# Gated mix on one core: halves of the tokens' tiles joined, spill, zero stores and weight loads moved

## The chip, the core and the metric

The kernel runs on one core of a Trainium2 chip. The metric is device time in microseconds. The kernel before took 444.37 us (median of 3 runs, 443.2 to 444.62).

Engines are named as in the profile: PE is the matmul engine (PEld its weight loads), DVE the vector engine, ACT the scalar engine, POOL the GpSimd engine, SP the engine that here issues every DMA. Each takes its instructions in order; a "q" behind the name (SPq, DVEq) is its queue.

## The reference

For 2048 tokens x of width 448, a gate mixes a sliding, dilated attention with a squared-ReLU MLP:

```python
g = sigmoid((x * gate_w).sum(-1, keepdims=True))
# attention: 16 heads of 28; query s sees keys s, s-2, ..., s-14
q, k, v = split(x @ wqkv)
a = (softmax(mask(q . k[s - 2*w]) * 28**-0.5) @ v) @ wo
# MLP, hidden width 1792
b = relu(x @ w1 + b1)**2 @ w2 + b2
out = g * a + (1 - g) * b
```

## The kernel before

**High and low parts.** PE multiplies in fp32r. To keep accuracy each operand is split in two: ACT rounds it to a high part (L101), DVE subtracts that from the original for the low part (L102), and a product takes three matmuls (high x high, high x low, low x high). The 448 rows of a contraction are three tiles of 128 and one of 64; the last 64 rows are stored twice, so that their parts share a tile. A chunk of 512 tokens therefore has eight tiles of x, `x0` to `x7`, each 128 x 512: high and low of three row tiles, and `x7`, `x8` for the rest (`X`, L113).

**Stage A, q, k, v.** Four chunks. The first (`qkv_first`, L235) runs while its weights still arrive, behind warm-up matmuls on a tile of zeros (L482). The others go through `qkv_two` (L262) twice each. Two products of 64 rows run side by side in the halves of PE; when an accumulator changes halves, a `turn` (L177) writes one element of its PSUM tile, by ACT (L182) or DVE (L184), which orders the two halves' matmuls. A finished accumulator is evacuated by ACT into a stage tile (L193, ring of `ST_BUFS = 3`); when two token tiles are in it, SP stores it to DRAM (`q_d`, `k_d`, `v_d`, L199).

**Spill.** The x tiles of chunks 0, 1 and 2 are stored to `x_d` (`x_spill`, L127) and loaded again in stage B (`x_reload`, L604) into a ring of `RING` buffers, of which `RING - 8` are loaded ahead of a chunk's end and the rest as its last matmuls free them.

**Attention** runs beside PE's work: POOL multiplies (L306 for q with k, L313 for weights with v), DVE reduces (L307, L319), ACT takes the exponential. Its q, k and v come from DRAM, shifted by the halo; rows before the first token are zeros, stored by `halos` (L540) from a tile `halo0`. Products go through a ring of `PP_BUFS = 4` tiles.

**Stage B, the MLP.** Chunks in the order 3, 0, 1, 2. For each of 14 hidden tiles f: eleven matmuls (`mlp_h`, L620), ACT's ReLU and squares (L626 to L628), DVE's low part hl (L629), and, two f later, twelve matmuls with w2 (`mlp_o`, L684). From the third chunk on, the attention output is transposed (L702, L703), split, and multiplied by wo (`wo_tr`, `wo_mm`, L725), one token tile per f as long as there are any; the last eight come in the tail.

**Order of work.** One Python program emits all engines' instructions, so what it emits first stands first in each engine's queue. A planner's clock counts PE's matmuls (`advance`, L431); `when(t, ...)` and `at(dt, ...)` put a load or a split at a time of this clock, in nanoseconds. `SPLIT_AT` sets the splits of the x chunks, `ATT_DELAY` when attention's first step is emitted after its loads. w1 arrives in four pieces (`w1_piece`, L454), w2's first seven rows in two (`w2_piece`), the other seven and wo row by row in stage B (`w2_row`, `wo_row`). The raw pieces of stage A share two buffers (`raw_tile`).

## Time and profile before

| | us |
|---|---|
| runs (3): lowest, median, highest | 443.2, 444.37, 444.62 |
| the profiled execution | 443.05 |
| its span | 441.3 |
| PE idle before an instruction, in the middle of the span | 3.6, 0.5 and 0.4 |

The page gives busy times per engine and the span in 40 slices of 11 us, of which these rows show the course:

```profile
PE   8969999999999999999999999999999999999996
DVE  4412312297899997776655677652857766663453
POOL 1000000784999899999898897843699998692000
PEclk9998999999999999999999999999999999999999
DMA  6899499979481304723203472210353600400013
```

A digit is the busy share in tenths. PE is busy nearly throughout, with a dip in the third slice; PEclk, the clock that PE was granted, dips in the fourth. DMA is busy above all in the first eleven slices, stage A. POOL begins with attention in the eighth and is done five slices before the end.

The DMAs that the change touches (out<-in, queue, count, KB each, median us from issue to landing):

```profile
x_d<-x SPq DMA_DIRECT2D x24, 256.0 KB, 7.3
q_d<-st SPq DMA_DIRECT2D x8, 448.0 KB, 6.0
w1raw<-w SPq DMA_DIRECT2D x4, 896.0 KB, 8.4
k_d<-st SPq DMA_DIRECT2D x8, 448.0 KB, 3.6
```

### The profile page before, as it was taken

What the parts mean: (1) busy time and instruction counts of PE and PEld (TensorE: products, weight loads), DVE (VectorE), ACT (ScalarE), POOL (GpSimd) and SP (SyncE); (2) the same over time, 40 slices, a digit from 0 to 9 for tenths busy, and PEclk for the clock granted to TensorE, in tenths of its full rate; (3) what the DMA queues carried; (4) which work ended last, traced back from release to release, by engine and by line L of the source; (5) the groups of instructions that cost most, each with busy time, mean ns of one, the idle gap of its engine ahead of it and who ended that gap; (6) DMA issues with size and microseconds to landing.
All of it is one profiled execution on the core that took longest, in us unless ns stands there. A gap on an engine that the chain in (4) does not pass through costs nothing.

```text
span 441.3 us, 6590 instructions
## 1 busy us (share of the span) xinstructions
PE 431.4 (98%) x2516; PEld 386.1 (87%) x2516; DVE 268.0 (61%) x384; ACT 178.6 (40%) x372; POOL 276.3 (63%) x167
## 2 busy tenths in 40 slices
PE   8969999999999999999999999999999999999996
PEld 7859999999888888888888888988888888888995
DVE  4412312297899997776655677652857766663453
ACT  4533453334475453344333552425333334333630
POOL 1000000784999899999898897843699998692000
PEclk9998999999999999999999999999999999999999
DMA  6899499979481304723203472210353600400013
GB/s 179 274 366 338 138 367 311 345 262 304 148 285 54 120 1 121 272 80 120 78 1 120 144 273 88 95 42 22 127 196 102 224 1 0 142 0 0 2 62 126
DMA packets 36623, 65.44 MB, mean 148 GB/s; under 512 B 3056, under 2 KB 26608, under 8 KB 36208
## 3 DMA queue, kind: packets, MB, share of 16 engines
q1 hardware_dynamic: 36592, 65.02, 43.2%
q8 instruction: 20, 0.33, 0.3%
q14 instruction: 11, 0.09, 0.1%
HBM read 41.23 MB, written 23.77 MB: 147 GB/s over the span
## 4 chain that ended last, share of the span: by engine, by line
PE 86%; DMA 5%; POOL 4%; DVE 2%; issue 1%; SPq 1%; ACT 1%; DVEq 0%; POOLq 0%; ACTq 0%
PE b L684 31%; PE h L620 30%; PE qkv L174 13%; PE a L725 8%; POOL qk L306 4%; DMA x_d<-x 2%; PE qkv L242 2%; DMA k<-k_d 1%; DMA q_d<-st 1%; PE oT L702 1%; PE warm L485 1%; DVE w2al L102 1%; SPq L502 1%; DVE lg L307 0%; ACT st L193 0%
## 5 line engine op out<-in xcount | busy, mean ns | idle before, releaser
L306 POOL TENSOR_TENSOR qk<-q,k 128x896 f32<-128x896 f32 x64 | 140.5, 2230 | 102.3 <-DMA k<-k_d 84.2
L313 POOL TENSOR_TENSOR av<-lg,v 128x896 f32<-128x896 f32 x64 | 122.6, 2018 | 13.3 <-DVE o L319 6.6
L626 ACT ACTIVATE h<-h,b1t 128x512 f32<-128x512 f32 x56 | 37.0, 661 | 164.9 <-PE h L620 164.9
L174 PE MATMUL qkv<-wqh,x 64*128 64x448 f32 (+1 forms) x528 | 88.3, 369 | 4.1 <-DVE qkv L184 3.6
L629 DVE TENSOR_TENSOR hl<-h,hh 128x512 fp32r<-128x512 f32 x56 | 38.5, 688 | 59.0 <-ACT h L628 58.9
L307 DVE TENSOR_REDUCE lg<-qk 128x32 f32<-128x896 f32 x64 | 67.1, 1076 | 0.5 <-POOL qk L306 0.5
L174 PEld LDWEIGHTS qkv<-wqh,x 64*128 64x128 f32 x528 | 60.7, 188 | 6.7 <-DVE qkv L184 4.3
L319 DVE TENSOR_REDUCE o<-av 128x112 f32<-128x896 f32 x64 | 66.4, 1073 | 0.1
L174 PE MATMUL qkv<-wql,x 64*128 64x448 f32 (+1 forms) x264 | 57.6, 368 | 0.0
L193 ACT ACTIVATE st<-qkv 128x448 f32<-128x448 f32 x48 | 24.7, 546 | 44.3 <-PE qkv L174 34.6
L684 PE MATMUL b<-w2ah,hl 128*128 128x448 f32 x112 | 40.7, 363 | 0.4 <-DVE hl L629 0.4
L684 PE MATMUL b<-w2bh,hh 128*128 128x448 f32 x112 | 41.0, 366 | 0.0
L684 PE MATMUL b<-w2bl,hh 128*128 128x448 f32 x112 | 40.9, 365 | 0.0
L684 PE MATMUL b<-w2bh,hl 128*128 128x448 f32 x112 | 40.9, 365 | 0.0
L684 PE MATMUL b<-w2ah,hh 128*128 128x448 f32 x112 | 40.7, 364 | 0.0
L684 PE MATMUL b<-w2al,hh 128*128 128x448 f32 x112 | 40.5, 362 | 0.0
L627 ACT ACTIVATE hh<-h 128x512 fp32r<-128x512 f32 x56 | 33.5, 599 | 3.6 <-DMA v_d<-st 1.8
L628 ACT ACTIVATE h<-h 128x512 f32<-128x512 f32 x56 | 33.2, 593 | 0.0
L174 PEld LDWEIGHTS qkv<-wql,x 64*128 64x128 f32 x264 | 31.8, 188 | 0.7
L620 PE MATMUL h<-x1b,w1h 128*128 128x512 f32 x84 | 28.6, 394 | 0.0
L620 PE MATMUL h<-x2b,w1h 128*128 128x512 f32 x84 | 28.5, 393 | 0.0
L620 PE MATMUL h<-x0b,w1h 128*128 128x512 f32 x84 | 28.4, 391 | 0.0
(108 smaller groups left out, 771.9 us busy)
## 6 DMA issues: line engine op xcount, KB each, us to landing
k<-k_d SPq DMA_DIRECT2D x8, 840.0 KB, 5.6
v<-v_d SPq DMA_DIRECT2D x8, 840.0 KB, 4.5
x_d<-x SPq DMA_DIRECT2D x24, 256.0 KB, 7.3
q_d<-st SPq DMA_DIRECT2D x8, 448.0 KB, 6.0
w1raw<-w SPq DMA_DIRECT2D x4, 896.0 KB, 8.4
k_d<-st SPq DMA_DIRECT2D x8, 448.0 KB, 3.6
v_d<-st SPq DMA_DIRECT2D x8, 448.0 KB, 6.9
q<-q_d SPq DMA_DIRECT2D x8, 448.0 KB, 3.4
```

The source lines that it names most:

```text
L174: nc.tensor.matmul(acc.pt[:, :acc.n], a[rows], w[rows], start=acc.todo == 21, stop=acc.todo == 1)
L306: nc.gpsimd.tensor_mul(pr, q[:, s:s + 1].to_broadcast([P, W, C]), k[:, s:s + W])
L307: pending.append(lambda: nc.vector.tensor_reduce(lg[:, s], pr.rearrange("p w (h d) -> p w h d", h=HG), axis=AX.X, op=ALU.add))
L313: nc.gpsimd.tensor_mul(pr.rearrange("p (h d) w -> p w h d", h=HG), lg[:, s][:, :, :, None].to_broadcast([P, W, HG, DH]), v[:, s:s + W].rea ...
L319: pending.append(lambda: nc.vector.tensor_reduce(o[:, g * C:(g + 1) * C], pr, axis=AX.X, op=ALU.add))
L620: nc.tensor.matmul(pt, w, a, start=i == 0, stop=i == len(pr) - 1)
L626: nc.scalar.activation(pt, pt, AF.Relu, bias=b1t[:, f:f + 1])
L627: nc.scalar.activation(hh, pt, AF.Square)
L628: nc.scalar.activation(pt, pt, AF.Square)
L629: at(HL_DELAY, lambda: nc.vector.tensor_sub(hl, pt, f32(hh)))
L684: nc.tensor.matmul(bps[tl][:, :D], a[:, sl], w, start=f == 0 and i == 0, stop=f == NF - 1 and i == 2)
L725: nc.tensor.matmul(pa[:, :D], a, w, start=i == 0, stop=i == len(pr) - 1)
```

## The change

- The high and the low part of a row tile of x lie in one tile, 128 x 2 x 512. A chunk has four tiles instead of eight, a spill four stores of 512 KB instead of eight of 256 KB, a reload four loads. `RING` is 5 of the new tiles instead of 10 of the old.
- Chunk 0's spill is emitted at 10.5 us of the planner's clock instead of 9, behind q's two stores on SP.
- The warm-up's `zero` lies in the ring of attention's products instead of in the buffer of k, to which k's weights are loaded.
- The zeros of the halo are stored by two DMAs instead of four, at 44.5 us instead of 16.
- w1's pieces, the biases and w2 come at other times; only four of w2's rows come in stage A, ten in stage B, one every 4.5 us instead of 3.2, and wo from 50 us into stage B instead of 26.
- `ATT_DELAY` is 20 us instead of 15.

```diff
-ATT_DELAY = 15000.0
+ATT_DELAY = 20000.0
-RING = 10
+RING = 5
-    x_d = tc.dram_tile([3, 8, P, CH], F32, name="x_d")
+    x_d = tc.dram_tile([3, 4, P, 2, CH], F32, name="x_d")
...
-            self.h, self.l = tiles[0:6:2], tiles[1:6:2]
-            self.x7, self.x8 = tiles[6:8]
+            self.h, self.l = [t[:, 0] for t in tiles[:3]], [t[:, 1] for t in tiles[:3]]
+            self.x7, self.x8 = tiles[3][:, 0], tiles[3][:, 1]
-        return X([pool.tile([P, CH], F32R, tag=f"x{j}", name=f"x{c}_{j}") for j in range(8)])
+        return X([pool.tile([P, 2, CH], F32R, tag=f"x{j}", name=f"x{c}_{j}") for j in range(4)])
...
-        split_full(raw[:, k], *(x.t[2 * k:2 * k + 2]))
+        split_full(raw[:, k], x.t[k][:, 0], x.t[k][:, 1])
     def x_spill(c, x):
-        for j in range(8):
+        for j in range(4):
             nc.sync.dma_start(x_d[c, j], f32(x.t[j]))
...
-    halo0 = smp.tile([G * HALO, C], F32, tag="lg", name="halo0")
+    halo0 = smp.tile([2 * G * HALO, C], F32, tag="lg", name="halo0")
...
-    zero = attp.tile([P, 2 * P], F32R, tag="k", name="zero")
+    zero = prodp.tile([P, 2 * P], F32R, tag="pp", name="zero", bufs=PP_BUFS)
...
-        for par in range(2):
-            for d in (k_d, v_d):
-                nc.sync.dma_start(d[par, :, 0:HALO], halo0)
+        for d in (k_d, v_d):
+            nc.sync.dma_start(d.rearrange("a g r c -> (a g) r c")[:, 0:HALO], halo0)
...
-    when(9000.0, x_spill, 0, x)
-    when(15000.0, w1_piece, 0, 13000.0)
-    when(16000.0, halos)
-    when(36500.0, w1_piece, 1, 10000.0)
-    when(48000.0, biases)
-    when(57500.0, w1_piece, 2, 11000.0)
-    when(67500.0, w1_piece, 3, 12000.0)
-    when(77500.0, w2_piece, 0, 4, w2ah, w2al, 0, 10000.0)
-    when(89000.0, w2_piece, 4, 3, w2ah, w2al, 0, 11000.0)
+    when(10500.0, x_spill, 0, x)
+    when(25000.0, w1_piece, 0, 13000.0)
+    when(44500.0, halos)
+    when(46500.0, w1_piece, 1, 12500.0)
+    when(67000.0, w1_piece, 2, 10500.0)
+    when(68000.0, w1_piece, 3, 17000.0)
+    when(70000.0, biases)
+    when(86000.0, w2_piece, 0, 4, w2ah, w2al, 0, 6500.0)
...
-        r = (8 * i + j) % RING
-        xt = (xpool if r < 8 else bp).tile([P, CH], F32R, tag=f"x{r}", name=f"x{c}b_{j}")
+        r = (4 * i + j) % RING
+        xt = (xpool if r < 4 else bp).tile([P, 2, CH], F32R, tag=f"x{r}", name=f"x{c}b_{j}")
...
-        at(5000.0, lambda: split_full(raw, w2bh[:, f - NFA], w2bl[:, f - NFA], soon))
+        at(5000.0, lambda: split_full(raw, *w2hl(f), soon))
...
-    for i in range(7):
-        at(i * 3200.0, lambda i=i: w2_row(NFA + i))
+    for i in range(4, NF):
+        at((i - 4) * 4500.0, lambda i=i: w2_row(i))
     for k in range(4):
-        at(26000.0 + k * 3200.0, lambda k=k: wo_row(k))
+        at(50000.0 + k * 4500.0, lambda k=k: wo_row(k))
...
-    early = RING - 8
+    early = RING - 4
...
-                nxt += [x_reload(i + 1, j) for j in range(early, 8)]
+                nxt += [x_reload(i + 1, j) for j in range(early, 4)]
```

## The prediction

> **What bounds the kernel now.** I read the page's busy times first, then PE's waits, then the chain of waits in order of time, and then the stretches around each wait.

> ```profile
> PE 431.4 (98%) x2516; PEld 386.1 (87%) x2516; DVE 268.0 (61%) x384; ACT 178.6 (40%) x372; POOL 276.3 (63%) x167
> ```

> PE is busy 431.4 of 441.3 us, and the change leaves its useful matmuls as they are. Only the 9.9 us in which PE is idle, and time in which it runs slowly, can be won. PE's waits:

> ```profile
> PE qkv L174 <- DVE qkv L184: 3.6, 1, 3.6
> PE warm L485 <- DVE zero L483: 1.2, 1, 1.2
> PE qkv L174 <- ACT qkv L182: 0.5, 1, 0.5
> PE b L684 <- DVE hl L629: 0.4, 1, 0.4
> ```

> The 3.6 us wait stands at 29.48 to 33.04. The chain says what it is made of (start, us, what):

> ```profile
> 15.08 8.74 DMA x_d<-x
> 23.88 5.67 DMA q_d<-st
> 30.09 0.97 ACT st L193 x2
> 31.07 0.53 ACT x L101
> 31.62 1.35 DVE x L102 x3
> 33.04 57.13 PE qkv L174 x536
> ...
> 121.44 2.55 DVE w2al L102
> 123.99 0.61 DVE hl L629
> ```

> Eight spill stores of chunk 0 hold the queue to 23.9, so q's first store is issued only then and lands at 29.6. ACT cannot evacuate k before that, for the stage ring has three buffers; behind that evacuation on ACT stand chunk 1's splits, behind those on DVE the memset of a turn, and PE waits for the memset. After the wait PE runs slowly for a while (columns: stretch, then busy time of PE, PEld, DVE, ACT, POOL, then the granted clock, DMA share, GB/s):

> ```profile
> 34.00:38.00 4.00, 4.00 (x28) 3.60 (x26) 0.22 (x3) 0.98 (x2) 0.00 (x0) 0.57 0.88 265
> ```

> At a clock of 0.57 over 4 us, 0.43 x 4 = 1.7 us of matmul time are lost. The half-microsecond wait belongs to another queue:

> ```profile
> SPq L502 <- PE warm L245: 5.4, 1, 5.4
> ```

> ```profile
> 16.31 0.58 ACT L101 ACTIVATE wqh<-wqraw 128x448 fp32r<-128x448 f32 x1 [1.15 <-DMA wqraw<-wqkv]
> ```

> SP waits 5.4 us to load k's weights, because the warm-up's `zero` lies in the buffer that they go to. They reach ACT late, and ACT's turn (L182), queued behind their split, is late for PE.

> **The change, part by part.** Times are sums against the profiled execution: 443.05 us, of which 441.3 are the span. That is 1.3 below the median of 444.37 shown; the forecast is moved by that difference at the end.

> *q's stores ahead of the spill.* q's two stores are then issued when ACT has evacuated them, at 17.5 to 18.9, not at 23.9. With the landing time of before, 5.67 us, the first lands near 23.2. From that landing to PE's restart the chain takes 33.04 - 29.57 = 3.5 us, so PE could go on at 26.7; it arrives at the turn at 29.5. The wait goes whole, with some 2.3 us to spare after the next item: 3.56 us, and with the idleness the slow stretch, 1.7 us. [...]

> What is late next is the spill itself: four stores of 512 KB, issued after q, with k's stores behind them on SP. The third stage buffer comes free for the last v tiles when k's first store has landed: issued near 25, landing after 4.4 us (median around there) to 8.7 us (the spills' median): 29 to 34. PE needs those PSUM tiles freed only 21 matmul pairs into chunk 1, at 32.5 + 21 x 0.205 = 36.8. Nothing is paid.

> *`zero` in another pool.* Eight loads are issued up to 5.4 us earlier (six of k's and v's weights, their last rows, then chunk 1's x). ACT's waits of 2.83 and 1.15 us for them end and PE's 0.53 us goes. They enter the queue behind the loads that PE needs first, and the one queue's packets start in order of issue in the trace, so those are not delayed: 0, bound +0.3 (PE's weight loads wait 0.3 us there now).

> *Pairs in one tile.* Spills and reloads become 12 issues each of 512 KB instead of 24 of 256 KB; the bytes stay. A reload of 256 KB lands in 3.3 to 5.0 us (medians), a 1 MB load in 8.0; 512 KB lies between, and I take 5. A slot comes free with the third matmul of a chunk's last h group and is needed at the fourth of the next: 8 x 0.227 + 36 x 0.2025 + 3 x 0.227 = 9.8 us. That hides it up to 9.8; without that cover each of three boundaries would pay the 5 us. The reloads stand on SP behind a q and a k load that wait for POOL; those go out some 10 us before them now (166.5 against 176.6).

> *Halos and biases.* Four zero stores become two and move behind chunk 2's spill; they must land before attention's first k load, at 72 now. Biases go 22 us later, still 35 us ahead of the first use at 118. Both cost nothing while the SP queue runs ahead as it does; SP's stores behind them wait for PE anyway.

> *Weights spread out.* w1's four pieces load 10, 10, 9.5 and 0.5 us later by the planner's clock, and three w2 rows of stage A become rows of stage B, loaded every 4.5 us and split 5 us later. Row f is needed about 28 + (f - 4) x 4.94 us into stage B (its first use now is 28 us in) and is ready near 8 + (f - 4) x 4.5: 20 us of cover. wo is ready 70 us in; its first use is 152 in. What the splits cost is DVE's time:

> ```profile
> L102 DVE TENSOR_TENSOR w1l<-w1raw,w1h x12: 615/630/1555, 41.2 to 99.9; 128x448 fp32r<-128x448 f32 x12
> L102 DVE TENSOR_TENSOR w2al<-w2raw,w2ah x7: 625/1532/2550, 102.6 to 121.4; 128x448 fp32r<-128x448 f32 x7
> L102 DVE TENSOR_TENSOR w2bl<-w2raw,w2bh x7: 564/1790/2046, 126.1 to 148.4; 128x448 fp32r<-128x448 f32 x7
> ```

> The same subtraction takes 0.63 us while POOL rests and up to 2.55 while it works. At the end of stage A two of them (119.4 to 124.0) hold up the first hl: PE's 0.36 us. The change puts three splits fewer there and hl ahead of more of the reductions, so I count 0.36 as won. In the first chunk of stage B DVE is nearly full:

> ```profile
> 116.00:186.00 70.00, 69.64 (x325) 60.66 (x324) 63.77 (x70) 35.52 (x70) 67.06 (x37) 1.00 0.43 146
> ```

> 63.8 of 70 us; fourteen splits run there instead of thirteen, but spread over 65 us instead of 36. At the chunk's end, though, the last two wo splits now stand between the four final additions and chunk 1's first hl on DVE. They add 0.6 to 2.1 us each, and the first hl is 2.8 us ahead of PE now (done 191.0, needed 193.8). So 0 to 1.5 us of new waiting; I take 0.6, nearer to the lower end because POOL, out of product buffers while DVE waits for the additions, mostly rests then.

> *ATT_DELAY.* Attention's steps are put 5 us later relative to PE's in the order of DVE and ACT. POOL itself starts when k lands, and does so earlier, as PE's stages end earlier. wo's transposes move one f step back; in the tail the first now comes after the MLP's matmuls and directly before the second, so a[0] waits for its evacuation. Transpose start to evacuated is 411.06 to 412.15 and two transposes take 0.88 us, then the low part comes about 0.35 us behind: +0.55 us, between 0.3 and 1.0.

> Sum: -3.56 - 1.7 - 0.53 - 0.36 + 0.6 + 0.55 = -5.0. 443.05 - 5.0 = 438.05, and on the median 439.4.

> **Rivals.** (1) *The stall is only shortened.* q's stores could land later behind the earlier loads: 1.57 MB of weights and 1 MB of x. For it: the DMA share is 1.0 from 15 to 30. Against it: these loads start 5 us earlier too, and moving the stores ahead takes 2 MB from before them. Half the stall left is 1.8 us: 441.2 if the clock stays up, as it did behind the waits of 0.53 and 0.36 us (granted 1.00), 442.9 if it falls as behind the 3.56. (2) *DVE is the bound at the end of stage A* (the slower side). In chunk 3 ten splits and four reductions (1.08 us each) stand before the last turn's memset, which PE needs 20.9 us after the first of them can begin. That is (20.9 - 4.3)/10 = 1.66 us a split. Below it nothing happens; at 2.3, as the pair at 119.4 took, PE stalls 10 x 0.64 = 6.4 us and pays 1.7 for the clock: 439.4 + 8.1 = 447.5. For it: DVE is busy 5.00 of 5.00 us in two stretches there now, and one memset came 0.2 us ahead of its need. Against: the six w1 subtractions from 87 to 99 averaged 1.5 (1.07, 1.54, 1.55, 2.55, 0.76, 1.53), and POOL rests while unit 1's k is loaded. (3) *The change gains nothing*: the landing of the moved loads makes a new wait of the same size, w1's second raw buffer or attention's q, k, v, say: 444.4. Against: every one has over 10 us of cover above.

> **How the numbers follow.** Forecast 0.80, (1) 0.08, (2) 0.06, (3) 0.06. About 0.3%, 1.3 us, is what a measurement can tell from no change. Faster: forecast and (1), 0.88; same 0.06; slower 0.06. The forecast's own range: the waits' bounds (-0.9 to +1.5) and the spacing of matmuls, for the buffers get other addresses: groups of eleven L620 matmuls take 2.49 to 2.57 us in the chain, mean 2.53, so 56 groups may move by 2.2 us either way. As they hardly all fall on one side, 437 to 442 for the forecast alone; the whole range, 436.3 to 442.9, adds all that could be gained and takes in (1).

> **What would show it.** In the profile after: no PE wait on L184 near 29, granted clock 1.00 from 8 us on, q_d's stores ahead of x_d's; no SP wait on L245's line; stage B beginning near 110 instead of 116; PE busy 98 to 99% of a span near 436. Wrong, if PE's waits name a DVE memset near 90 to 108, a reload at a chunk's boundary, or an hl in stage B with more than 2 us, or if PE's busy time itself grows.

## The result and the profile after

| | before | after |
|---|---|---|
| median of the runs on one chip (4 each), us | 443.78 (442.64 to 444.62) | 436.53 (436.45 to 436.64) |
| profiled execution, us | 443.05 | 436.64 |
| its span, us | 441.3 | 434.9 |
| start of stage B, us | 116.11 | 109.60 |

The ratio after to before is 0.9838, with a 95% interval of 0.9813 to 0.9864: the changed kernel is faster by 1.4 to 1.9%. The forecast was 439.4 in a range of 436.3 to 442.9. Lines of stage A are numbered two higher in the changed kernel (L174 is L176, L184 is L186); from L601 on they are the same.

From the page of the kernel after (busy us, share of the span; the two rows are the 40 slices; then the shares of the chain that ended last):

```profile
span 434.9 us, 6554 instructions
PE 429.1 (99%) x2516; PEld 385.9 (89%) x2516; DVE 257.9 (59%) x384; ACT 179.3 (41%) x372; POOL 274.8 (63%) x167
...
PE   8999999999999999999999999999999999999996
...
PEclk9999999999999999999999999999999999999999
...
PE 97%; DMA 1%; DVE 1%; SPq 0%; issue 0%; ACT 0%
```

The dip in PE's third slice and the one of the clock in the fourth are gone. The chain is PE's own work to 97%, where it was 86%. Of PE's waits (engine, line, whom it waited for: total, times, longest) the one of the warm-up on its zeros, which stands at the very start, is all that is left:

```profile
PE warm L487 <- DVE zero L485: 1.2, 1, 1.2
```

Why nothing is waited for near 29 us is read from the SP queue of the kernel after (start, us, line, out<-in, count):

```profile
5.90 4.19 SPq L504 DMA_DIRECT2D wqraw<-wqkv  x6
...
11.43 0.33 SPq L479 DMA_DIRECT2D xraw<-xT  x1
15.97 1.46 SPq L201 DMA_DIRECT2D q_d<-st  x2
17.49 4.18 SPq L131 DMA_DIRECT2D x_d<-x  x4
24.43 0.92 SPq L201 DMA_DIRECT2D k_d<-st  x2
```

k's and v's weights go out at 5.9, without SP's wait of 5.4 us; q's stores go out at 16.0 where they went at 23.9, and the spill stands behind them. What that leaves in hand is on DVE, kernel after (the bracket is the idle time before an instruction and what ended it):

```profile
25.39 1.93 DVE L102 TENSOR_TENSOR x<-xraw,x 128x512 fp32r<-128x512 f32 x3 [4.48 <-ACT x L101]
26.68 0.06 DVE L186 MEMSET qkv<- 1x1 f32 x2
27.25 0.68 DVE L102 TENSOR_TENSOR x<-xraw,x 128x512 fp32r<-128x512 f32 x1
28.76 0.09 DVE L186 MEMSET qkv<- 1x1 f32 x2 [0.83 <-PE qkv L176]
```

The two memsets for which PE stood still from 29.5 to 33.0 are now done at 26.74. PE comes to that turn at 28.55, so they are 1.8 us early; the next two wait for PE.

Where the 6.4 us between the profiled executions went can be counted to about 0.1 us. Undisturbed matmul pairs of stage A start 0.205 us apart; every larger distance, less 0.205, is time lost there, and the like holds for stage B with its own distances. Against the prediction's terms:

| place | lost before, us | lost after, us | predicted difference, us |
|---|---|---|---|
| memset of the turn near 29 | 3.82 | 0 | -3.56 |
| slow matmuls at 34.4 to 37.7 | 1.55 | 0 | -1.7 |
| ACT's turn near 16 | 0.80 | 0 | -0.53 |
| a turn at 96.5, barely late | 0.28 | 0 | not in the sum |
| first hl of stage B | 0.62 | 0 | -0.36 |
| chunk 1's first hl | 0 | 0 | +0.6 |
| tail's first transposes | 0 | 0.7 | +0.55 |
| sum | 7.07 | 0.7 | -5.0 |

7.07 - 0.7 = 6.37, and the executions differ by 443.05 - 436.64 = 6.41. The stage A rows make 6.45, and stage B begins 116.11 - 109.60 = 6.51 us sooner; it is then as long as before (325.3 us against 325.2), since what it gains at the first hl it pays in the tail. "Chunk 1" in these rows is, as in the prediction, the second chunk of stage B.

### The profile page after: what moved, and what is told of

Read it like the earlier page. It is cut to its first block, busy times and chain, and to the rows that moved or that the text cites. A ratio compares the mean times of both kernels' runs of the same rounds, so it can differ in the third digit from the quotient of the medians.

```text
span 434.9 us, 6554 instructions
## 1 busy us (share of the span) xinstructions
PE 429.1 (99%) x2516; PEld 385.9 (89%) x2516; DVE 257.9 (59%) x384; ACT 179.3 (41%) x372; POOL 274.8 (63%) x167
## 4 chain that ended last, share of the span: by engine, by line
PE 97%; DMA 1%; DVE 1%; SPq 0%; issue 0%; ACT 0%
PE h L620 33%; PE b L684 31%; PE qkv L176 22%; PE a L725 8%; PE oT L702 1%; PE qkv L244 1%; DMA xraw<-xT 1%; PE oT L703 0%; SPq L499 0%; SPq L494 0%; DVE bt L660 0%; DVE wql L513 0%; DVE x L514 0%; DVE ol L102 0%; ACT o L101 0%
## 5 line engine op out<-in xcount | busy, mean ns | idle before, releaser
L308 POOL TENSOR_TENSOR qk<-q,k 128x896 f32<-128x896 f32 x64 | 138.6, 2193 | 103.4 <-DMA k<-k_d 72.5
L176 PE MATMUL qkv<-wqh,x 64*128 64x448 f32 (+1 forms) x528 | 86.8, 363 | 0.0
L629 DVE TENSOR_TENSOR hl<-h,hh 128x512 fp32r<-128x512 f32 x56 | 38.6, 688 | 62.1 <-ACT h L628 61.9
L309 DVE TENSOR_REDUCE lg<-qk 128x32 f32<-128x896 f32 x64 | 66.9, 1076 | 3.9 <-POOL qk L308 3.9
L176 PEld LDWEIGHTS qkv<-wqh,x 64*128 64x128 f32 x528 | 59.6, 185 | 0.6
L176 PE MATMUL qkv<-wql,x 64*128 64x448 f32 (+1 forms) x264 | 56.5, 363 | 0.0
L684 PE MATMUL b<-w2bl,hh 128*128 128x448 f32 x112 | 40.9, 365 | 0.0
L684 PE MATMUL b<-w2bh,hl 128*128 128x448 f32 x112 | 40.9, 365 | 0.0
L684 PE MATMUL b<-w2bh,hh 128*128 128x448 f32 x112 | 40.9, 365 | 0.0
L684 PE MATMUL b<-w2ah,hh 128*128 128x448 f32 x112 | 40.7, 364 | 0.0
L684 PE MATMUL b<-w2ah,hl 128*128 128x448 f32 x112 | 40.6, 362 | 0.0
L684 PE MATMUL b<-w2al,hh 128*128 128x448 f32 x112 | 40.5, 362 | 0.0
L176 PEld LDWEIGHTS qkv<-wql,x 64*128 64x128 f32 x264 | 30.8, 185 | 0.3
L620 PE MATMUL h<-x1b,w1h 128*128 128x512 f32 x84 | 28.6, 395 | 0.0
L620 PE MATMUL h<-x2b,w1h 128*128 128x512 f32 x84 | 28.5, 393 | 0.0
L620 PE MATMUL h<-x0b,w1h 128*128 128x512 f32 x84 | 28.4, 391 | 0.0
```

The lines of the kernel that those rows point to most:

```text
L176: nc.tensor.matmul(acc.pt[:, :acc.n], a[rows], w[rows], start=acc.todo == 21, stop=acc.todo == 1)
L308: nc.gpsimd.tensor_mul(pr, q[:, s:s + 1].to_broadcast([P, W, C]), k[:, s:s + W])
L309: pending.append(lambda: nc.vector.tensor_reduce(lg[:, s], pr.rearrange("p w (h d) -> p w h d", h=HG), axis=AX.X, op=ALU.add))
L620: nc.tensor.matmul(pt, w, a, start=i == 0, stop=i == len(pr) - 1)
L629: at(HL_DELAY, lambda: nc.vector.tensor_sub(hl, pt, f32(hh)))
L684: nc.tensor.matmul(bps[tl][:, :D], a[:, sl], w, start=f == 0 and i == 0, stop=f == NF - 1 and i == 2)
```

## The experiments

All ratios are to the kernel before on the same chip, with 95% intervals. The kernel before scatters far more than the changed one (442.98 to 446.66 over these chips' runs), so the intervals are between +-0.14% and +-0.38%, 0.6 to 1.7 us.

### One part alone, and both moves undone

Four kernels, to tell which part removes the wait at 29.

e1_order_only, on the kernel before:

```diff
-    when(9000.0, x_spill, 0, x)
+    when(10500.0, x_spill, 0, x)
```

> The kernel before with one edit: chunk 0's spill emitted behind q's two stores. Theory A (the order on SP made the stall): q's first store lands near 23.5, PE's wait at 29.5 and the slow stretch behind it go, 3.8 + 1.55 = 5.4 us less; the 0.8 us at 16 stays: 437.6 against a profiled 443.05. Theory B (what delayed everything was SP's wait for the warm-up's zero): part of the stall stays, 439 to 442.

e2_zero_only, on the kernel before:

```diff
-    zero = attp.tile([P, 2 * P], F32R, tag="k", name="zero")
+    zero = prodp.tile([P, 2 * P], F32R, tag="pp", name="zero", bufs=PP_BUFS)
```

> The kernel before with one edit: the warm-up's zero in the ring of products. Theory A: only the 0.8 us at 16 goes, 442.3, for q's stores still stand behind the spill. Theory B: SP is 3 to 5 us earlier with all that follows, the spill too, q's first store lands near 24 and PE's long wait goes with it: 436.8.

e3_pairs_only, on the kernel before:

```diff
...
-        return X([pool.tile([P, CH], F32R, tag=f"x{j}", name=f"x{c}_{j}") for j in range(8)])
+        return X([pool.tile([P, 2, CH], F32R, tag=f"x{j}", name=f"x{c}_{j}") for j in range(4)])
...
-        for j in range(8):
+        for j in range(4):
             nc.sync.dma_start(x_d[c, j], f32(x.t[j]))
...
```

> The kernel before with the high and low part of x in one tile (half as many spills and reloads), nothing else. Theories A and B: SP gets to q's stores some 4 us earlier, but the queue's packets come in order behind the same 2 MB, so that the store lands at most 1 us earlier: 442 to 443. Theory C (the number of issues was the delay): the stall shrinks by 2 to 4 us and the clock stays up, 438 to 440.

e4_undo_both, on the kernel after:

```diff
-    when(10500.0, x_spill, 0, x)
+    when(9000.0, x_spill, 0, x)
...
-    zero = prodp.tile([P, 2 * P], F32R, tag="pp", name="zero", bufs=PP_BUFS)
+    zero = attp.tile([P, 2 * P], F32R, tag="k", name="zero")
```

> The changed kernel with the spill's old place and the zero's old buffer. If these two edits are the whole gain: wait and slow stretch return, 442 to 443. If the pairs or the weights' times carry a part of it: 438 to 441.

| kernel | median, us | ratio | lost at 29 | lost later in stage A |
|---|---|---|---|---|
| e1_order_only | 442.98 | 0.9949 [0.9929, 0.9970] | none | 0.7 at 65; 4.1 at 82.6, then a lowered clock (mean of the execution 0.990) |
| e2_zero_only | 437.93 | 0.9840 [0.9805, 0.9875] | 0.1 | 2.4 at 81.1 and a half clock from 83.4 to 86.8 |
| e3_pairs_only | 444.83 | 0.9992 [0.9972, 1.0012] | 4.7 | lowered clock behind it (mean of the execution 0.991) |
| e4_undo_both | 442.77 | 0.9954 [0.9936, 0.9972] | 4.8 | half clock from 31.9 to 38.8 |

The number of DMAs alone does nothing: e3 keeps the stall. It even shows that the time of q's issue isn't the whole matter. The chain of e3 (start, us, what):

```profile
19.10 12.36 DMA q_d<-st
...
34.95 1.11 PE qkv L174 x3
```

Here SP, with four spill issues in place of eight, issues q's store at 19.1 and not at 23.9, but it lands 12.4 us later, at 31.46, where the one of before landed at 29.6. The spill's bytes are ahead of it in the queue either way.

The order and the zeros, each alone, remove the wait at 29. That was not expected of both: the two moves are two cures of one wait, not two terms of a sum. But a wait of the same kind comes further on. PE's waits on the turns' memsets, in e1:

```profile
PE qkv L174 <- DVE qkv L184: 4.5, 2, 4.0
```

in e2:

```profile
PE qkv L174 <- DVE qkv L184: 2.2, 1, 2.2
```

and the chain that leads to that of e2:

```profile
63.72 6.24 DMA v_d<-st
...
70.44 10.28 DMA w1raw<-w
...
80.74 0.59 ACT w1h L101
...
82.53 1.07 DVE lg L307
83.61 0.06 DVE w1l L102
83.66 0.04 DVE qkv L184
...
83.72 11.44 PE qkv L174 x87
```

w1's third piece is issued at 70.44, right behind attention's load of v on SP, which goes out when a store of v has landed (63.72 + 6.24), and the piece lands at 80.7. Its splits stand on DVE ahead of the turn's memset, and PE needs that at 81.1. In the kernel before the same memset came only at 87.33, but PE, held up by 3.82 + 1.55 + 0.80 = 6.2 us until then, did not wait for it. So the losses near 16 and 29 had covered a second one. In e2 it did not cost every execution the same: the profiled one took 439.74 at a mean granted clock of 0.996, the other three 437.3 to 438.2 at 1.000.

### Which part keeps the second wait away

e5_after_old_weights, on the kernel after (all due times of weights, halos and biases as before, and ATT_DELAY):

```diff
-ATT_DELAY = 20000.0
+ATT_DELAY = 15000.0
...
-    when(67000.0, w1_piece, 2, 10500.0)
+    when(57500.0, w1_piece, 2, 11000.0)
...
```

> The changed kernel (pairs, spill at 10500, zeros in the product pool) with all due times of weights, halos and biases and ATT_DELAY (15000) as before. Theory D (the long wait at 29 is cured by the zeros' pool or the spill's place, but PE, some 5 us earlier, then meets a second wait near 82, because three splits of w1's third piece stand in VectorE's order ahead of the last two memsets of the round, and that piece is loaded only behind attention's first loads): no wait at 29, a wait of 1.5 to 4 us on VectorE's memset at 80 to 84, slow matmuls behind it, median 437.5 to 440. Rival G (spills in half as many DMAs get the third piece out in time, old due times or not): no wait of over 0.3 us, stage B beginning near 109.7, median 435.8 to 436.8.

e6_after_att15000, on the kernel after, and e8_after_att17000 likewise with 17000.0:

```diff
-ATT_DELAY = 20000.0
+ATT_DELAY = 15000.0
```

> The changed kernel with ATT_DELAY 15000 alone, as before. Theory D (the weights' due times cure the wait at 82; ATT_DELAY has no part in it): stage A without a wait over 0.3 us; and the tail's first two transposes stand apart again, which wins back the 0.66 us that the changed kernel lost there: median 435.9 (435.4 to 436.3). Rival H (ATT_DELAY is what keeps VectorE's reduces of attention out from in front of the round's last memsets): a wait of 1 to 4 us near 80 to 84 with slow matmuls behind it, median 437.5 to 440.

> The changed kernel with ATT_DELAY 17000, the latest of the values tried at which PE's order keeps the tail's first two transposes apart. If the tail's 0.66 us is paid for that order alone: median 435.9 (435.5 to 436.2). Rival: it is paid for attention's end (POOL), which comes no earlier: 436.5, as the changed kernel.

e7_zero_w1split, on the kernel before, with the zeros moved as in e2 and:

```diff
-    when(57500.0, w1_piece, 2, 11000.0)
+    when(57500.0, w1_piece, 2, 15500.0)
```

> The kernel before with two lines changed: the zeros in the product pool, and the splits of w1's third piece due 4500 later (15500 in place of 11000), which puts them behind the round's last two memsets in VectorE's order. Theory D: neither the wait at 29 nor the one at 82, stage B beginning near 109.7, the tail as in the kernel before: median 436.2 (435.4 to 436.9). Rival F (fewer DMAs, or the wider spread of loads, are needed for the gain): another wait of 1 us or more somewhere in stage A, or late hl tiles in stage B; median 437.5 or more.

| kernel | median (runs), us | ratio | lost in the profiled execution, us |
|---|---|---|---|
| e5_after_old_weights | 437.23 (436.7 to 437.87) | 0.9823 [0.9786, 0.9861] | 0.9 at 81, 0.3 at 91, 1.1 at the first hl, tail 0 |
| e6_after_att15000 | 436.89 (435.25 to 438.15) | 0.9817 [0.9787, 0.9846] | 1.4 at 92, first hl 0, tail 0 |
| e7_zero_w1split | 441.18 (439.16 to 442.12) | 0.9908 [0.9875, 0.9941] | 1.2 at 90, 1.2 at 93, 1.0 at the first hl, tail 0 |
| e8_after_att17000 | 436.16 (435.43 to 436.71) | 0.9803 [0.9774, 0.9832] | 0.3 at 92, first hl 0, tail 0 |

e5 falls between its two theories. The wait near 82 is there, as the order on DVE demands, but only a third as long as in e2 (0.7 against 2.2 us), and the clock stays up (0.999 in the mean): the piece goes out at 68.92 and lands at 78.54, 2.2 us sooner than in e2. The weights' times are thus one part of the cure, and what e5 has beyond e2 (half the DMAs, the spill behind q) another; which of these two it is was not taken apart. PE's waits in e5 show what else the spread of the weights does:

```profile
PE b L685 <- DVE hl L630: 0.8, 1, 0.8
PE qkv L176 <- DVE qkv L186: 0.7, 1, 0.7
```

The wait on stage B's first hl is back, and it is absent in e6: between these two the weights' times remove it, not ATT_DELAY. The old times don't always bring it, though: e1 and e2 have them and lose nothing at the first hl, behind their stalls at 82.

e6 shows what ATT_DELAY does. There is no wait at 82, as theory D said, and the tail is whole again, but 1.4 us are lost at 92, which neither theory had. It comes from one subtraction. From the groups of DVE's line L102 between 60 and 110 us (minimum, median, maximum in ns), and from POOL's timeline, both e6:

```profile
L102 DVE TENSOR_TENSOR w1l<-w1raw,w1h x9: 609/626/5326, 65.3 to 99.8; 128x448 fp32r<-128x448 f32 x9
```

```profile
83.10 8.41 POOL L308 TENSOR_TENSOR qk<-q,k 128x896 f32<-128x896 f32 x4
```

The subtraction starts at 86.66 and ends at 91.99, 0.5 us after the last of POOL's four products (91.51). Its median is 0.63 us. In the kernel after the longest is 2.55 us: it starts at 87.35, POOL's product ends at 89.42, and it is done at 89.89. In e8 one takes 4.26. The two reductions (L309) that run beside these four products before it, at 83.18 and 85.29, keep their 1.09 us. In e9 the subtraction starts at 87.13, POOL's four products end at 92.25, and it is done at 92.73. So what was left of POOL's run when the subtraction started was 2.07 us in the kernel after, 4.85 in e6 and 5.12 in e9, and it took 2.55, 5.33 and 5.60: each time it ended 0.5 us behind the run, in the first behind the rest of one product, in the other two behind the rest of one and two more. When POOL's run ends follows from the program: each product takes one of four buffers (`PP_BUFS`), and DVE's reductions, which free them, stand behind the subtraction that is held up. In the kernel after and in e9 DVE had done three reductions of this unit, and POOL stopped after its seventh product, 3 + 4; in e6 it had done five, and POOL went on to the unit's eighth and last.

e7 went against theory D: with the splits of the third piece due later, the waits at 29 and 82 are both gone, but the later splits now meet attention's reductions and POOL's products (1.5 to 2.1 us each for the four from 83.4 to 92.9, then 0.61 to 0.64), and PE waits twice near 90 to 94 and at the first hl. The profiled execution is the fastest of its six, so what cost the others up to 3 us more isn't seen. Moving one split is not the weights' spread.

In e8 the tail's loss is gone, as forecast (the distances of the first tail matmuls are those of the kernel before), and the span is 434.4 against 434.9. The intervals overlap (0.9774 to 0.9832 here, 0.9813 to 0.9864 for the changed kernel), and the two medians, 436.16 and 436.53, are of different chips. It may be 0.4 us faster; that isn't shown.

### Each move undone alone, and the margin

e9_undo_zero and e10_undo_order, on the kernel after, are the two halves of e4's edit.

> The changed kernel with the zeros back in attention's pool (tag k) alone; the spill stays behind q's stores. If the two moves are two cures for the one wait at 29, and the other one is enough: no wait near 29, at most the 0.5 us wait near 16 back, median 436.5 to 437.3. Rival (both are needed in the changed kernel; the margin is too small for one): a wait of 1 us or more near 29, median 438.5 to 441.

> The changed kernel with x's first spill back ahead of q's first stores (due at 9000) alone; the zeros stay in the product pool. If the two moves are two cures for the one wait: no wait near 29, median 436.3 to 436.9. Rival (both are needed): a wait of 1 us or more near 29, median 438.5 to 441.

e11_stall_1us and e12_stall_2us, on the kernel after, repeat the first copy of chunk 1's split six and eight times more, which writes the same values again; the edit of e11 is shown, e12's has 8 in place of 6:

```diff
+            def part(c, k):
+                for r in range(6 if c == 1 and k == 0 else 0):
+                    nc.scalar.activation(xs[c].t[0][:, 0], xraw[c][:, 0], AF.Copy)
+                x_split(xraw[c], xs[c], k)
-            when(t + k * 900.0, lambda c, k: x_split(xraw[c], xs[c], k), c, k)
+            when(t + k * 900.0, part, c, k)
```

> The changed kernel with the first copy of chunk 1's split done seven times instead of once: six more copies on ScalarE (6 x 0.53 = 3.2 us) ahead of VectorE's splits and the turn's memsets. The memset needed by TensorE at 28.55 was there at 26.7, so a margin of 1.8 is left: a wait of 1.3 us (1.0 to 1.6) near 28.5. Theory W (the clock is halved for one window of 3.41 us behind each window of that length in which TensorE was idle for about 1.8 to 2.0 us or more, the windows running on from where the clock first rose): no half clock in any run, median 437.8 (437.5 to 438.2), runs within 0.5 of each other. Rival K (the clock follows a stall's own length, with a limit above 1.5): the same here. Rival M (the margin is smaller, as the profile shows only one run): a wait of over 2 us, median over 439.

> The same with eight more copies (4.2 us): a wait of 2.4 us (2.1 to 2.7). Theory W: whether the clock drops depends on where the windows' edges fall in the stall, so from run to run: times in two groups, about 438.9 without and about 440.4 with a half window, the range of the runs over 1.0 us. Rival K (a stall's own length decides, limit between 1.5 and 2.6): all runs in one group, within 0.5 us, at either 438.9 or 440.4.

| kernel | median (runs), us | ratio | PE's waits, us |
|---|---|---|---|
| e9_undo_zero | 438.67 (436.14 to 438.88) | 0.9837 [0.9811, 0.9864] | 0.4 at 16, none at 29, 1.3 at 93 |
| e10_undo_order | 437.26 (436.51 to 438.26) | 0.9825 [0.9808, 0.9843] | 0.7 at 28 |
| e11_stall_1us | 440.39 (440.38 to 440.46) | 0.9895 [0.9881, 0.9909] | 2.1 at 28.5, then half clock |
| e12_stall_2us | 442.93 (441.53 to 444.19) | 0.9951 [0.9934, 0.9968] | 3.4 at 28.8, then half clock; 0.8 at 192, the first hl of the second chunk |

With the new load times either move will do for the wait at 29: e9 and e10 can't be told from the changed kernel by their ratios, while e4, without both, loses 72% of the gain (0.46 of 1.62%), and e1, with the order but the old load times, nearly as much. Each leaves something, though. In e9 the whole SP queue runs later (k's and v's weights at 11.2, not 5.9; w1's last pieces at 76.4, not 73.3), and a subtraction of 5.60 us beside POOL costs 1.6 at 93. In e10 q's store has the spill ahead of it, and the chain is the old one, shortened:

```profile
15.68 9.95 DMA q_d<-st
...
29.12 3.96 PE qkv L176 x35
```

e11 confirms the margin. The copies take 0.66 us each in a row, not the 0.53 that I had reckoned with, so 3.95 us were put in; ACT's timeline and PE's waits of e11:

```profile
24.56 3.95 ACT L559 ACTIVATE x<-xraw 128x512 fp32r<-128x512 f32 x6
```

```profile
PE qkv L176 <- DVE qkv L186: 2.1, 1, 2.1
```

3.95 - 2.1 = 1.85 against the 1.8 read from the profile after. The expected 1.3 us of wait was off by the copies' price alone. But the clock fell, which decides something about the clock (last section). The cost agrees: 2.1 of wait and half of a 3.41 us stretch, 1.7, make 3.8; the profiled executions differ by 440.38 - 436.64 = 3.74. (The medians differ by 3.86, but they are of different chips.)

In e12 the runs lie at 441.53, at 442.74 to 443.19 (four) and at 444.19. They are neither the two groups of theory W at 438.9 and 440.4 nor the one narrow group of rival K. But both forecasts were for a wait of 2.4 us, and it came to 3.4, so neither was put to the test; and the wait at 192 was in neither. In e11, where by W about half of the runs should have kept the clock, all four lost it (mean granted clocks of 0.994 to 0.996, against 0.998 to 1.000 for the changed kernel), which four runs can do by chance. So these two don't settle whether the windows' edges or the length of the stall decides.

## Why the prediction was right

**The mechanism and its chain.** Right: no wait on L186 near 29, granted clock 1.00 from 6.3 to 433.0 us, q's stores first on SP, stage B from 109.60 (110 was named), a span of 434.9 (near 436), PE at 99%. The stall went whole and not by half, as rival (1) would have it, with 1.8 us to spare where the prediction counted 2.3 after the zeros' share.

**The credit.** Here the step failed, though the sum didn't feel it. "q's stores ahead of the spill" was credited with the whole wait and the slow stretch, and "`zero` in another pool" with PE's half microsecond alone. e2 shows that the zeros' move removes the wait at 29 by itself, and brings, in the kernel before, a gain that can't be told from the whole change (0.9840 against 0.9838). The path is in the prediction's own numbers: the eight loads go out up to 5.4 us earlier, and so does all that stands behind them on SP. In e2 q's first store goes out at 19.0, with the spill still ahead of it, and lands 5.8 us later, at 24.8 and not at 29.6; in e1 it goes out at 17.8 and lands after 6.3. The two terms overlap, and the whole was booked under one.

**What hides behind the stall.** "Weights spread out" was costed at -0.36 and +0.6, and "ATT_DELAY" at the tail alone. The -0.36 was right in kind (measured -0.62; e5 against e6 shows that it is the weights' times). Missed was what e1, e2 and e5 show: with the old times, PE, some 6 us earlier, outruns w1's third piece and stalls at 82. With both moves made the new times can't be told from the old ones by the median (e5 0.9823); with the order alone they, the pairs and ATT_DELAY together are worth two thirds of the gain (e1 0.9949, e9 0.9837). I had asked what the moved loads would make late, not what the unmoved ones would.

**Chunk 1's first hl.** "0 to 1.5, I take 0.6" for two wo splits ahead of it: nothing was lost. The risk was real, though. In the profile after, one of these splits takes 2.48 us, and the hl is done at 185.5 and needed at 186.6, so that of the 2.8 us of cover before 1.1 are left. In e12 PE waits 0.8 us for it:

```profile
PE b L688 <- DVE hl L633: 0.8, 1, 0.8
```

With this term at 0 the sum is -5.6; the rest of the way to -6.4 is under-counted idleness (0.26 at 29, 0.27 at 16, 0.26 at the first hl) and the turn at 96.5, less 0.15 each in the clock's and the tail's term.

**The tail.** +0.55, between 0.3 and 1.0; measured 0.7, in the place named. The profile after, PE's timeline:

```profile
404.24 0.27 PE L703 MATMUL oT<-ident,od 128*128 128x128 f32 x1
404.66 0.47 PE L725 MATMUL a<-woh,oh 128*128 128x448 f32 x1
404.96 0.37 PE L725 MATMUL a<-wol,oh 128*128 128x448 f32 x1
405.42 0.47 PE L725 MATMUL a<-woh,ol 128*128 128x448 f32 x1
```

Starts of 0.42, 0.30 and 0.46 us apart where a matmul takes 0.20: PE waits for the transposes' evacuation and then for its low part. e6 and e8 put the transposes apart and have none of it. The spacing of matmuls, for which the range allowed 2.2 us either way, did not move: stage B without these waits takes the same time to 0.1 us. No run shows that the buffers' addresses change it, as the range supposed.

**Rival (2), DVE late at the end of stage A,** had the right place. It didn't come in the changed kernel (the memsets at 90.89 and 92.48 were in time), but in e6 and e9 a subtraction of 5.3 to 5.6 us beside POOL cost 1.4 to 1.6 us there. The cover is thinner than the weight of 0.06 suggested.

**The median.** Of the 2.9 us between 439.4 and 436.53, 1.4 are the terms above and 1.4 the step "the forecast is moved by that difference": the profiled execution of before was 1.3 below its median, and I carried that over. The changed kernel's profiled execution is 0.1 above its median, and its four runs lie within 0.2 us.

**The clock behind a shorter stall.** The slow stretch was put at 1.7 us and had cost 1.55. Rival (1) left open whether the clock stays up behind half the stall, 1.8 us. No run has a wait of that length: behind 1.1 us in e6 and 1.3 in e9 the granted clock stayed at 1.00, and behind 2.1 us in e11 it was 0.50 for 3.41 us in the profiled execution, with a mean of 0.994 to 0.996 in all four of its runs.

## What to carry to other kernels

When a stall on the critical engine is removed, everything behind it is needed earlier by the stall's length: go through the later waits of that engine and subtract it from their margins, those that the change doesn't touch too. Two edits that each free the same queue are alternatives, so their gains are not to be added; ask of each what it does without the other. And a profiled execution's distance from its median belongs to that kernel's scatter: don't carry it over to the changed kernel.

## What the runs showed of the hardware

```profile
24.20:27.61 3.41, 3.41 (x36) 1.00 1.06 392
27.61:31.02 3.41, 1.88 (x20) 1.00 1.01 342
31.02:34.43 3.41, 1.39 (x14) 1.00 0.97 326
34.43:37.85 3.42, 3.42 (x22) 0.50 0.87 253
```

and e11:

```profile
27.70:31.11 3.41, 1.32 (x14) 1.00 1.00 327
31.11:34.52 3.41, 3.41 (x20) 0.50 0.04 14
34.52:37.93 3.41, 3.41 (x36) 1.00 0.60 215
```

A stretch in which PE was idle for 2.02 (before), 2.09 (e11) or 1.87 us (e2) is followed by one at a granted clock of 0.50, in which PE is busy again but, in the kernel before, starts its matmul pairs 0.37 us apart and not 0.205; the first stretch of the stall before, with 1.53 us idle, is not, nor are those of e6 (1.07) and e9 (1.29). Cut in the same way, the profiles of e4 and e12 fit: stretches with 3.05 (e4) and 3.06 us idle (e12) are followed by half clock, and so is one with 1.63 us in e4, which was itself at half clock. None of these stretches was idle as a whole: PE was busy for at least 0.35 us of each. In a stretch at full clock, 1.87 us of idleness was followed by the half clock, and 1.53 was not. In the kernel before the clock fell at such a step, 34.43, 1.4 us after PE had resumed (33.04). Whether only the share of the stretch counts stays open: the stalls that were followed by half clock were also the longest ones, and e11 and e12 did not part the two.

**A split's subtraction took from 0.6 to 5.6 us,** ending 0.5 us behind POOL's run of products where it was longest (2.55 us in the kernel after, beside one product; 5.33 in e6 and 5.60 in e9, beside three); reductions beside POOL's products in the same stretch kept 1.08 to 1.09 us (e6, e9).

**A store's landing went by the bytes ahead of it more than by its issue:** in e3 q's store, with the spill's 2 MB ahead of it as before, was issued 4.8 us earlier and landed 1.9 us later, 12.4 us after its issue; in e10, with the spill ahead of it, it took 9.95 us, in e1, with the spill behind, 6.3.
